# Attention scores by head on half the partitions, and value products of the first units in 32-column pieces, in an attention plus feed-forward kernel

## The chip, the cores and the metric

The kernel runs on one core of a Trainium2 chip. The metric is the device time of one execution in microseconds (us); the time before is the median of three runs. A profile is one execution taken by the hardware profiler. In it PE is TensorE (PEld its weight loads), DVE is VectorE, ACT is ScalarE, POOL is GpSimd and SP is SyncE, whose queue issues all the DMAs here.

## The reference

Chunked attention with a few memory keys, and behind it a two-layer feed-forward net on the result. Everything is float32.

```python
B, H, S, D = 4, 8, 768, 64            # batch, heads, sequence, head size; chunk 32, left 16, right 8, n_mem 8
for c in range(S // 32):              # a chunk of 32 queries sees 8 memory keys and up to 56 keys around it
    k_full = concat([mem_k, k[:, :, l_start:r_end]]);  v_full = concat([mem_v, v[:, :, l_start:r_end]])
    scores = (q_c @ k_full.T) / sqrt(D)
    a = exp(scores - max(scores));  a = a / (sum(a) + 1e-9)
    out[:, :, c_start:c_end] = a @ v_full
x = out.transpose(0, 2, 1, 3).reshape(3072, 512)
h = x @ w_in                          # 512 x 2048
g = maximum(h, 0) + alpha * minimum(h, 0)
return g @ w_out                      # 2048 x 512
```

## The kernel before

The 3072 tokens are cut into 8 blocks of 384 (`BT`). A block has 4 attention **units**, each a pair of heads, so there are 32 units; a unit's result is 128 rows of x (two heads of 64) by 384 tokens. The feed-forward net works through 16 pieces `f` of the hidden size for each block. For a piece, `up` (L581) makes h of 128 hidden rows by 384 tokens in 12 matmuls, since each operand is split into a high and a low part and three of the four products are added; ACT and DVE bend it (`sides`, `join`, `high`, `low`), and `down` (L613) adds 9 matmuls of 128 by 512 to the block's output in three PSUM banks. These split products run in fp32r; the products of attention are plain float32.

A unit's **scores** (`score_products`, L269) are 12 matmuls: 4 groups `g` of 32 output partitions times 3 slots `n`. A chunk has 32 queries, so a matmul writes 32 partitions. Its moving operand is 128 columns, 64 keys for each of two heads. The keys lie in `kbs`, which has a plane for each head with zeros on the other head's 64 partitions, so one matmul over 128 rows gives both heads. The zeros are written once by memsets (L189, L190), and the keys come in two DMAs of 64 partitions each (`load_k`, L235).

The **first 8 units** (blocks 0 and 1, `windows`, L407) run before the feed-forward net has anything to do and go another way than the 24 later ones. DVE takes the maximum (L417) and subtracts it (L421), ACT exponentiates, DVE sums (L429), inverts (L435) and scales the weights (L438), TensorE transposes them into the bank `t_ps` (L445), ACT copies them out (L450), and 24 matmuls of 64 output columns make the **values** (`values`, L460) in `a_ps`. `xh` and `xl` (L386, L390) are the two parts of x. A few matmuls on a constant tile (`stir`, L254) stand ahead of scores and transposes. In the later units the scores are exponentiated in six pieces on ACT (L299), GpSimd scales (L318), DVE transposes in 32 x 32 squares (L339), and 8 matmuls make the values (L353).

The 8 PSUM banks: two for h, three for the output of a block (`o0`, `o1`, `o2` in `ps_o`), two for scores (`s0`, `s1` in `ps_s`), one for values (`a`). The first units' scores all use `s0` and their transposes `s1`; later units alternate between the two. Blocks 0 and 1 share the weights as these arrive (`ORDER`, `NJOINT`): block 1's first 9 pieces accumulate in `s0`, `s1` and `a`.

The order of the work is not the order of the code. Each step is handed to a planner (`Plan`) with its engine, an assumed cost, what it reads and writes, and a due time; the planner walks a list schedule and writes each engine's instructions in that order. A change of a cost, a key or a due time so moves instructions everywhere. A later unit begins at the feed-forward step that `BEGIN` or `LATER` names; its weights are due `DUE_WEIGHTS` steps on, and its values stand `DUE_VALUES` steps on. Weights of the net arrive as bit patterns and are decoded by ACT and DVE (`decode_part`, L523 to L550) before they can be used. All DMAs stand in SP's queue in the planner's order.

Of the kernel before, what the change touches and what calls it, by code (L numbers as in the profile page):

```python
# [78 lines left out]
BEGIN = {2: (2, 4, 6, 8)}  # L79
# [5 lines left out]
DUE_WEIGHTS, DUE_VALUES = 2, 4  # L85
# [67 lines left out]
def body(ctx: ExitStack, tc: tile.TileContext, qvw, kw, vw, w_in, w_out, alpha, out):  # L153
# [23 lines left out]
    kbs = [const.tile([P, 2, NT, NKT], F32, name=f"kb{i}") for i in range(NKB)]  # L177
# [3 lines left out]
    spare = [wps[f, 0].tile([P, 2 * NT * NKT + BT], F32, name="early", tag="w") for f in (NF - 1, NF - 2)]  # L181
    kbs += [t[:, :2 * NT * NKT].rearrange("p (h t k) -> p h t k", h=2, t=NT) for t in spare]
    qs = [const.tile([P, BT], F32, name=f"q{i}") for i in range(2)] + [t[:, 2 * NT * NKT:] for t in spare]
# [42 lines left out]
    def load_unit(u):  # L226
        blk, pr = divmod(u, NPAIR)
        state[u] = {}
        i = sets(u)

        def load_q():
            nc.sync.dma_start(out=qs[i], in_=qvw[blk, pr, :, :BT])

        def load_k(h2):
            nc.sync.dma_start(out=kbs[i][h2 * D:(h2 + 1) * D, h2], in_=kw[blk, pr, h2 * D:(h2 + 1) * D])  # L235

        step(SP, 0.75, load_q, writes=[("q", i)], rest=due(u))
        for h2 in range(2):
            step(SP, 0.55, partial(load_k, h2), writes=[("k", i, h2)], rest=due(u))
# [16 lines left out]
    def score_products(u):  # L256
        blk, pr = divmod(u, NPAIR)
        st = state[u]
        k = u % 2 if u >= NWIN else 0
        s_ps = ps_s.tile([P, 512], F32, name="s_ps", tag=f"s{k}")  # L260
        if u < NWIN:
            stir(s_ps, STIR[0] if u == 0 else STIR[1])
        st["s"] = s_ps[:, :NJ * 2 * KW].rearrange("p (n h k) -> p n h k", n=NJ, h=2)
        st["sg"] = s_ps[:, :NJ * 2 * KW].rearrange("p (n k) -> p n k", k=KW)
        for n in range(NJ):
            for g in range(4):
                t, j = SLOT[(g, n)]
                c = t * NJ + j
                nc.tensor.matmul(  # L269
                    out=st["s"][g * CH:(g + 1) * CH, n],  # L270
                    lhsT=qs[sets(u)][:, c * CH:(c + 1) * CH],
                    rhs=kbs[sets(u)][:, :, t, STARTS[j]:STARTS[j] + KW],
                    start=True, stop=True,
                )
# [9 lines left out]
    def scores(u):  # L284
        st = state[u]

        def top():
            hide(u)
            st["mx"] = sm.tile([P, NJ * 2], F32, name="mx", tag=f"mx{u % 3}")
            nc.vector.tensor_reduce(out=st["mx"], in_=st["sg"], axis=AX.X, op=ALU.max)  # L290
# [4 lines left out]
        def exps(i):  # L295
            if i == 0:
                st["e"] = at.tile([P, NJ * 2, KW], F32, name="e", tag=f"e{u % 2}")
                st["den"] = sm.tile([P, NJ * 2, 1], F32, name="den", tag=f"den{u % 3}")
            nc.scalar.activation(out=st["e"][:, i], in_=st["sg"][:, i], func=AF.Exp, scale=SCALE,  # L299
                                 bias=st["mx"][:, i:i + 1], accum_out=st["den"][:, i])  # L300

        step(DVE, 0.66, top, writes=[("s", u % 2), ("mx", u % 3)], rest=due(u))
        step(DVE, 0.16, negate, writes=[("mx", u % 3)], rest=due(u))
        for i in range(NJ * 2):
            step(ACT, 0.54, partial(exps, i), reads=[("s", u % 2), ("mx", u % 3)],
# [54 lines left out]
    def attend(place, olds, news):  # L360
# [11 lines left out]
        for u in news:  # L372
            reads += [("q", sets(u)), ("k", sets(u), 0), ("k", sets(u), 1)]
            writes += [("s", u % 2)]
        step(PE, 0.85 * len(olds) + 0.82 * len(news) - (0.2 if olds and news else 0.0), products, reads=reads, writes=writes,
# [25 lines left out]
    def load_windows(u):  # L401
# [5 lines left out]
        step(SP, 1.4, load, writes=vw_keys(u), rest=due(u))  # L407

    def windows(u):

        st = state[u]
        sk, tk = ("s", 0), ("s", 1)

        def top():
            hide(u)
            st["mx"] = sm.tile([P, NJ * 2, 1], F32, name="mx", tag=f"mx{u % 3}")
# [376 lines left out]
```

## Time and profile before

| | |
|---|---|
| runs | 622.9, 627.49, 624.33 us; median 624.33 |
| the profiled execution | 626.75 us, of which the span from the first to the last instruction is 625.0 |
| busy | PE 613.4 us (98%), PEld 538.2, DVE 404.1, ACT 261.6, POOL 25.0 |
| chain that ended last | PE 96%, DVE 2%; o_ps L613 43%, h_ps L581 42%, s_ps L269 4.1%, a_ps L353 3.1%, a_ps L460 1.8% |
| scores, all 32 units | L269 MATMUL, 672 + 96 records, 24.6 + 3.9 us busy |
| values, first 8 units | L460 MATMUL, 192 + 192 records, 6.8 + 6.4 us busy |

A float32 matmul leaves two records in the trace, so 12 matmuls of scores are 24 records. Matmul records overlap, since they are pipelined: what a block of them costs is read from the start of its first record to the start of what follows. A `[x <- y]` behind a row is the idle time of that engine before it, and who ended it.

### The profile page before, as it was taken

The page shows a single profiled execution, that of the slowest core. Times are in us where ns is not written, and L with a number is a line of the kernel's source. Part 1 is how long each engine was busy: PE and PEld are TensorE (multiplying, and loading weights), DVE is VectorE, ACT ScalarE, POOL GpSimd, SP SyncE. Part 2 cuts the span into 40 slices and gives each one's busy share as a digit, 9 for nine tenths or more (in the row PEclk, how much of TensorE's full clock was granted, in tenths as well). Part 3 has the DMA queues.
Part 4 walks back from the last instruction along what each step waited for, and adds up shares of the span by engine and source line. Part 5 has one row for each costly group of instructions (what it writes and reads, how often), then busy time and mean ns, then how long its engine had stood idle before and what let it go on. Part 6 is the DMA issues. An engine that isn't in the chain of part 4 may idle for free.

```text
span 625.0 us, 10996 instructions
## 1 busy us (share of the span) xinstructions
PE 613.4 (98%) x4278; PEld 538.2 (86%) x4278; DVE 404.1 (65%) x984; ACT 261.6 (42%) x716; POOL 25.0 (4%) x37
## 2 busy tenths in 40 slices
PE   6999999999999999999999999999999999999997
PEld 3688999988888889988888988888998888988996
DVE  6788888976975676665566665567666556633332
ACT  2478989764423323433324323342334332231212
POOL 1001000001000000000000000000000000000000
PEclk9898999999999999999999999999999999999999
DMA  8999800022312100311111111130013100010001
GB/s 231 283 404 409 277 1 1 2 62 73 122 46 71 47 29 21 99 49 49 47 46 54 48 49 47 48 99 23 27 49 98 49 18 18 2 51 1 2 0 50
DMA packets 22596, 48.43 MB, mean 77 GB/s; under 512 B 3088, under 2 KB 7184, under 8 KB 22544
## 3 DMA queue, kind: packets, MB, share of 16 engines
q1 hardware_dynamic: 22544, 47.73, 23.7%
q8 instruction: 33, 0.54, 0.4%
q14 instruction: 19, 0.16, 0.1%
HBM read 41.43 MB, written 6.29 MB: 76 GB/s over the span
## 4 chain that ended last, share of the span: by engine, by line
PE 96%; DVE 2%; issue 0%; ACT 0%
PE o_ps L613 43%; PE h_ps L581 42%; PE s_ps L269 4%; PE a_ps L353 3%; PE a_ps L460 2%; PE s_ps L254 1%; DVE pt L339 1%; PE t_ps L445 0%; PE t_ps L254 0%; DVE a L539 0%; ACT w_t L531 0%; DVE up L595 0%; DVE w L550 0%; DVE mx L417 0%; DVE w_t L535 0%
## 5 line engine op out<-in xcount | busy, mean ns | idle before, releaser
L581 PE MATMUL h_ps<-xh,w 128*128 128x384 f32 x1024 | 262.6, 337 | 0.9 <-DVE w L550 0.9
L613 PE MATMUL o_ps<-w,gh 128*128 128x512 f32 x768 | 239.8, 394 | 0.0
L581 PEld LDWEIGHTS h_ps<-xh,w 128*128 128x128 f32 x1024 | 186.7, 189 | 4.7 <-DVE w L550 1.2
L581 PE MATMUL h_ps<-xl,w 128*128 128x384 f32 x512 | 174.0, 340 | 0.5 <-DVE xl L390 0.5
L613 PEld LDWEIGHTS o_ps<-w,gh 128*128 128x128 f32 x768 | 144.1, 188 | 27.8
L591 ACT ACTIVATE up<-h_ps 128x384 f32<-128x384 f32 x128 | 63.2, 493 | 222.0 <-PE h_ps L581 217.6
L613 PE MATMUL o_ps<-w,gl 128*128 128x512 f32 x384 | 151.7, 395 | 0.1
L595 DVE SCALAR_TENSOR_TENSOR up<-dn,nal,up 128x384 f32<-128x384 f32 x128 | 79.3, 620 | 107.0 <-ACT dn L591 106.3
L339 DVE STREAM_TRANSPOSE pt<-e 32x192 f32<-32x192 f32 (+1 forms) x336 | 99.5, 301 | 9.8 <-POOL e L318 5.3
L581 PEld LDWEIGHTS h_ps<-xl,w 128*128 128x128 f32 x512 | 96.6, 189 | 5.9 <-ACT xh L386 0.8
L613 PEld LDWEIGHTS o_ps<-w,gl 128*128 128x128 f32 x384 | 72.1, 188 | 15.9 <-issue 3.6
L605 DVE TENSOR_TENSOR gl<-up,gh 128x384 fp32r<-128x384 f32 x128 | 71.2, 557 | 3.9 <-ACT gh L601 0.3
L591 ACT ACTIVATE dn<-h_ps 128x384 f32<-128x384 f32 x128 | 62.4, 488 | 0.0
L299 ACT ACTIVATE e<-s_ps,mx 128x64 f32<-128x64 f32 x144 | 43.2, 319 | 36.3 <-DVE mx L293 35.4
L601 DVE CAST gh<-up 128x384 fp32r<-128x384 f32 x104 | 36.5, 352 | 22.7 <-PE o_ps L613 16.8
L386 ACT CAST xh<-a_ps 128x384 fp32r<-128x384 f32 x32 | 15.3, 479 | 58.1 <-PE a_ps L353 50.0
L318 POOL TENSOR_TENSOR e<-e,den 128x384 f32<-128x384 f32 x24 | 20.3, 847 | 462.5 <-DVE den L315 438.8
L299 ACT ACTIVATION_READ_ACCUMULATOR e<-s_ps,mx 128x1 f32 x144 | 30.4, 211 | 0.0
L312 DVE TENSOR_SCALAR den<-den 128x6 f32<-128x6 f32 x24 | 4.1, 169 | 32.1 <-ACT e L299 32.1
L269 PE MATMUL s_ps<-kb,q 128*32 128x128 f32 x672 | 24.6, 280 | 0.0
L353 PEld LDWEIGHTS a_ps<-pt,v_t 128*64 128x64 f32 x384 | 16.6, 136 | 8.7 <-issue 8.7
L269 PEld LDWEIGHTS s_ps<-kb,q 128*32 128x32 f32 x672 | 17.2, 111 | 5.5 <-issue 2.1
(59 smaller groups left out, 312.2 us busy)
## 6 DMA issues: line engine op xcount, KB each, us to landing
w_t<-w_in SPq DMA_DIRECT2D x16, 512.0 KB, 10.1
w_t<-w_out SPq DMA_DIRECT2D x16, 512.0 KB, 10.0
kb<-kw SPq DMA_DIRECT2D x56, 136.0 KB, 3.1
v_t<-qvw SPq DMA_DIRECT2D x24, 256.0 KB, 2.7
out<-o_t SPq DMA_DIRECT2D x24, 256.0 KB, 2.1
q<-qvw SPq DMA_DIRECT2D x28, 192.0 KB, 3.1
vw<-vw SPq DMA_DIRECT2D x4, 384.0 KB, 6.6
early<-vw SPq DMA_DIRECT2D x4, 384.0 KB, 6.6
```

The source lines that it names most:

```text
L269: nc.tensor.matmul(out=st["s"][g * CH:(g + 1) * CH, n], lhsT=qs[sets(u)][:, c * CH:(c + 1) * CH], rhs=kbs[sets(u)][:, :, t, STARTS[j]:STAR ...
L299: nc.scalar.activation(out=st["e"][:, i], in_=st["sg"][:, i], func=AF.Exp, scale=SCALE, bias=st["mx"][:, i:i + 1], accum_out=st["den"][:, i])
L318: nc.gpsimd.tensor_tensor(out=st["e"], in0=st["e"], in1=st["den"].broadcast_to([P, NJ * 2, KW]), op=ALU.mult)
L339: nc.vector.transpose(out=pts[u % NPT][quad * CH:(quad + 1) * CH, j, t0:t0 + n1 - n0].rearrange("p t h q -> p (t h) q"), in_=(st["e"], zer ...
L353: nc.tensor.matmul(out=st["a"][h2 * D:(h2 + 1) * D, t * TQ:(t + 1) * TQ], lhsT=st["v"][:, t, h2, :], rhs=pts[u % NPT][:, :, t, h2, :], sta ...
L386: nc.scalar.copy(out=st["xh"], in_=st["a"][:, :BT])
L581: nc.tensor.matmul(out=h["ps"][:, :BT], lhsT=ws[f, 0][:, wk, k * P:(k + 1) * P], rhs=xs[first + k][xk], start=(k == 0 and n == 0), stop=(k ...
L591: nc.scalar.activation(out=h[name], in_=h["ps"][:, :BT], func=AF.Relu, scale=sign)
L595: nc.vector.scalar_tensor_tensor(out=h["g"], in0=h["dn"], scalar=nal[:, f:f + 1], in1=h["up"], op0=ALU.mult, op1=ALU.add)
L601: copy(out=h["gh"], in_=h["g"])
L605: nc.vector.tensor_tensor(out=h["gl"], in0=h["g"], in1=h["gh"].bitcast(F32), op=ALU.subtract)
L613: nc.tensor.matmul(out=o_ps[tt], lhsT=h[gk][:, tt * P:(tt + 1) * P], rhs=ws[f, 1][:, wk], start=(f == first_f and i == 0), stop=(f == last ...
```

## The change

It has these parts. (1) Scores go by head: 24 matmuls of 64 columns instead of 12 of 128, each on the 64 partitions of its head, without zeros; the two heads write two different PSUM banks (a tile of `[P, 2, 512]`). (2) `kbs` loses its second plane and the memsets, and a unit's keys come in one DMA on 128 partitions. (3) The first units' scores alternate between two pairs of banks, `ps_s` and the first two banks of `ps_o`, and their transposes use the third bank of `ps_o`; so block 0's first `down` has to wait for the last of these. Later units have one pair of banks in place of two single ones. (4) The first units' value products write 32 output columns at a time, 48 matmuls instead of 24. (5) The first units' weights are scaled by GpSimd instead of DVE. (6) The planner's costs and due times change: block 2's units begin one step later, weights are due one step later.

```diff
-BEGIN = {2: (2, 4, 6, 8)}
+BEGIN = {2: (3, 5, 7, 9)}
...
-DUE_WEIGHTS, DUE_VALUES = 2, 4
+DUE_WEIGHTS, DUE_VALUES = 3, 4
...
-    kbs = [const.tile([P, 2, NT, NKT], F32, name=f"kb{i}") for i in range(NKB)]
+    kbs = [const.tile([P, NT, NKT], F32, name=f"kb{i}") for i in range(NKB)]
...
-    for i, kb in enumerate(kbs):
-        eng = nc.gpsimd if i % 2 else nc.vector
-        eng.memset(kb[0:D, 1], 0.0)
-        eng.memset(kb[D:P, 0], 0.0)
...
-        def load_k(h2):
-            nc.sync.dma_start(out=kbs[i][h2 * D:(h2 + 1) * D, h2], in_=kw[blk, pr, h2 * D:(h2 + 1) * D])
-
-        step(SP, 0.75, load_q, writes=[("q", i)], rest=due(u))
-        for h2 in range(2):
-            step(SP, 0.55, partial(load_k, h2), writes=[("k", i, h2)], rest=due(u))
+        def load_k():
+            nc.sync.dma_start(out=kbs[i], in_=kw[blk, pr])
+
+        step(SP, 0.65, load_q, writes=[("q", i)], rest=due(u))
+        step(SP, 0.81, load_k, writes=[("k", i)], rest=due(u))
...
-        k = u % 2 if u >= NWIN else 0
-        s_ps = ps_s.tile([P, 512], F32, name="s_ps", tag=f"s{k}")
+        pair = (ps_o if u < NWIN and u % 2 else ps_s).tile([P, 2, 512], F32, name="s_ps", tag="s")
...
-                nc.tensor.matmul(
-                    out=st["s"][g * CH:(g + 1) * CH, n],
-                    lhsT=qs[sets(u)][:, c * CH:(c + 1) * CH],
-                    rhs=kbs[sets(u)][:, :, t, STARTS[j]:STARTS[j] + KW],
-                    start=True, stop=True,
-                )
+                for h2 in range(2):
+                    rows = slice(h2 * D, (h2 + 1) * D)
+                    nc.tensor.matmul(
+                        out=st["s"][g * CH:(g + 1) * CH, n, h2],
+                        lhsT=qs[sets(u)][rows, c * CH:(c + 1) * CH],
+                        rhs=kbs[sets(u)][rows, t, STARTS[j]:STARTS[j] + KW],
+                        start=True, stop=True,
+                    )
...
-            nc.vector.tensor_tensor(out=st["e"], in0=st["e"], in1=st["den"].broadcast_to([P, NJ * 2, KW]),
+            nc.gpsimd.tensor_tensor(out=st["e"], in0=st["e"], in1=st["den"].broadcast_to([P, NJ * 2, KW]),
...
-            st["t"] = ps_s.tile([P, 512], F32, name="t_ps", tag="s1")
+            st["t"] = ps_o.tile([P, 512], F32, name="t_ps", tag="a")
...
-                    for h2 in range(2):
+                    for h2, i in ((0, 0), (1, 0), (0, 1), (1, 1)):
                         rows = slice(h2 * D, (h2 + 1) * D)
                         nc.tensor.matmul(
-                            out=st["a"][rows, c * CH:(c + 1) * CH],
-                            lhsT=vws[u % NSET][rows, c, :],
+                            out=st["a"][h2 * D + i * CH:h2 * D + (i + 1) * CH, c * CH:(c + 1) * CH],
+                            lhsT=vws[u % NSET][rows, c, i * CH:(i + 1) * CH],
                             rhs=st["et"][rows, n, g * CH:(g + 1) * CH],
```

The planner's costs that change with it: a unit's scores 1.26 to 1.08 (first units) and 0.82 to 0.67 (later), values of the first units 1.55 to 0.95, scaling from DVE 0.55 to POOL 0.86, and the loads.

Place one, TensorE among the first units: the scores and values around the first transposes. Before:

```order
L254 MATMUL s_ps<-busy 128x512
L269 MATMUL s_ps<-early 32x128 x12
L460 MATMUL a_ps<-et,vw_162 64x32 x24
L254 LDWEIGHTS busy
L254 MATMUL t_ps<-busy 128x512
L445 MATMUL t_ps<-eye,e 128x128 x3
```

The same place in the changed kernel, where the fifth unit's scores stand ahead of the second unit's values:

```order
L249 MATMUL s_ps<-busy 128x512
L264 MATMUL s_ps<-kb_154,q_159 32x64 x24
L455 MATMUL a_ps<-et,vw_162 32x32 x48
L249 LDWEIGHTS busy
L249 MATMUL s_ps<-busy 128x512
```

Both blocks have twice the matmuls at half the size, and scores of the next units have moved ahead of transposes by about one unit.

Place two, DVE among the first units, from one unit's sum to the next unit's. Before, the scaling (L438) stands in DVE's row:

```order
L432 TENSOR_SCALAR den<-den 128x6
L280 MEMSET s_ps 32x2x16
L417 TENSOR_REDUCE mx<-s_ps 128x6
L435 RECIPROCAL den<-den 128x6
L421 TENSOR_TENSOR e<-s_ps,mx 128x384
L438 TENSOR_TENSOR e<-e,den 128x384
L429 TENSOR_REDUCE den<-e 128x6
```

Of the change, a little later, where the decoding of the net's first weights (L530, L534) stands between the units' steps:

```order
L427 TENSOR_SCALAR den<-den 128x6
L530 TENSOR_SCALAR w_t<-w_t 128x512
L430 RECIPROCAL den<-den 128x6
L534 SCALAR_TENSOR_TENSOR a<-a,w_t 128x512
L416 TENSOR_TENSOR e<-s_ps,mx 128x384
```

And GpSimd's whole row in the changed kernel from its first work on:

```order
L187 MEMSET eye 128x128
L188 ISA
L188 AFFINE_SELECT eye<-eye 128x128
L433 TENSOR_TENSOR e<-e,den 128x384 x8
L479 MEMSET e_1111 128x384
L482 MEMSET pt_1113 128x768
```

The eight scalings left DVE; behind a reciprocal, where GpSimd now starts, DVE goes on with whatever is next, here a decode step with two operands in SBUF. GpSimd's memsets of the later units' buffers stand behind the eight scalings.

Place three, TensorE at block 0's first `down`, with the numbers of the tiles (`o_ps_1033` is the pair of banks, `o_ps_1034` the third one, `t_ps_1015` and `a_ps_1051` belong to the last of the first units):

```order
L440 MATMUL t_ps_1015<-eye_156,e_844 128x128 x3
L609 MATMUL o_ps_1033<-w_941,gl_1023 128x512
L609 MATMUL o_ps_1033<-w_941,gh_1012 128x512 x2
...
L609 MATMUL o_ps_1034<-w_941,gl_1023 128x512
L609 MATMUL o_ps_1034<-w_941,gh_1012 128x512 x2
L455 MATMUL a_ps_1051<-et_1028,early_163 32x32 x48
```

Before, at the same place:

```order
L445 MATMUL t_ps_759<-eye_156,e_683 128x128 x3
L581 MATMUL h_ps_639<-xl_768,w_505 128x384
L581 MATMUL h_ps_639<-xh_764,w_505 128x384 x2
L613 MATMUL o_ps_780<-w_752,gl_770 128x512
L613 MATMUL o_ps_780<-w_752,gh_755 128x512 x2
L613 MATMUL o_ps_781<-w_752,gl_770 128x512
```

The first `down` stands behind the last transpose in both kernels; one quarter of an `up` has moved from ahead of it to behind the last values.

More of the change, by code (lines that the diff above doesn't have):

```diff
@@ L298, in exps @@
                 st["den"] = sm.tile([P, NJ * 2, 1], F32, name="den", tag=f"den{u % 3}")
-            nc.scalar.activation(out=st["e"][:, i], in_=st["sg"][:, i], func=AF.Exp, scale=SCALE,
-                                 bias=st["mx"][:, i:i + 1], accum_out=st["den"][:, i])
-        step(DVE, 0.66, top, writes=[("s", u % 2), ("mx", u % 3)], rest=due(u))
+            nc.scalar.activation(out=st["e"][:, i], in_=st["s"][:, i // 2, i % 2], func=AF.Exp, scale=SCALE,
+                                 bias=st["mx"][:, i // 2, i % 2:i % 2 + 1], accum_out=st["den"][:, i])
+        step(DVE, 0.66, top, writes=["s", ("mx", u % 3)], rest=due(u))
         step(DVE, 0.16, negate, writes=[("mx", u % 3)], rest=due(u))
         for i in range(NJ * 2):
-            step(ACT, 0.54, partial(exps, i), reads=[("s", u % 2), ("mx", u % 3)],
+            step(ACT, 0.54, partial(exps, i), reads=["s", ("mx", u % 3)],
                  writes=[("e", u % 2, i), ("den", u % 3, i)] if i else e_keys(u) + den_keys(u), rest=due(u))
@@ L372, in attend @@
         for u in news:
-            reads += [("q", sets(u)), ("k", sets(u), 0), ("k", sets(u), 1)]
-            writes += [("s", u % 2)]
-        step(PE, 0.85 * len(olds) + 0.82 * len(news) - (0.2 if olds and news else 0.0), products, reads=reads, writes=writes,
+            reads += [("q", sets(u)), ("k", sets(u))]
+            writes.append("s")
+        step(PE, 0.85 * len(olds) + 0.67 * len(news) - (0.2 if olds and news else 0.0), products, reads=reads, writes=writes,
              rest=rest(place))
@@ L465, in values @@
                         )
-        step(PE, 1.26, partial(score_products, u), reads=[("q", sets(u)), ("k", sets(u), 0), ("k", sets(u), 1)],
+        step(PE, 1.08, partial(score_products, u), reads=[("q", sets(u)), ("k", sets(u))],
              writes=[sk], rest=due(u))
@@ L474, in windows @@
         step(DVE, 0.19, inverse, writes=den_keys(u))
-        step(DVE, 0.55, scale, reads=den_keys(u), writes=e_keys(u))
+        step(POOL, 0.86, scale, reads=den_keys(u), writes=e_keys(u))
         step(PE, 0.68, turn, reads=e_keys(u) + ["eye"], writes=[tk], rest=due(u, 1))
         step(ACT, 0.48, keep, reads=[tk], writes=["e2"])
-        step(PE, 1.55, values, reads=["e2"] + vw_keys(u), writes=["a"], rest=due(u, 1))
+        step(PE, 0.95, values, reads=["e2"] + vw_keys(u), writes=["a"], rest=due(u, 1))
         split(u)
@@ L500, in load @@
             nc.sync.dma_start(out=raw[k][:, j].rearrange("p m b -> p (m b)"), in_=srcs[i][f])
-        after = {NF - 1: [("q", 2), ("k", 2, 0), ("k", 2, 1)], NF - 2: [("q", 3), ("k", 3, 0), ("k", 3, 1)],
+        after = {NF - 1: [("q", 2), ("k", 2)], NF - 2: [("q", 3), ("k", 3)],
                  NF - 3: [("vw", 2), ("vw", 3)]}.get(f, [])
         for i in range(2):
-            step(SP, 1.9, partial(load, i), writes=[("r", f, i)] + after, rest=rest(place_of(f)))
+            step(SP, 1.31, partial(load, i), writes=[("r", f, i)] + after, rest=rest(place_of(f)))
     def place_of(f):
@@ L608, in down @@
             if f == first_f:
-                banks = [(ps_o, f"o{i}") for i in range(NTT)] if not joint else [(ps_s, "s0"), (ps_s, "s1"), (ps_a, "a")]
-                o_ps.extend(pool.tile([P, DM], F32, name="o_ps", tag=tag) for pool, tag in banks)
+                pair = (ps_s if joint else ps_o).tile([P, 2, DM], F32, name="o_ps", tag="s")
+                last = (ps_a if joint else ps_o).tile([P, DM], F32, name="o_ps", tag="a")
+                o_ps.extend([pair[:, 0], pair[:, 1], last])
             for tt in range(NTT):
@@ L649, in keep @@
         for tt in range(NTT):
-            step(ACT, 0.58, partial(copy, tt), reads=[(("s", 0), ("s", 1), "a")[tt]],
+            step(ACT, 0.58, partial(copy, tt), reads=[("s", "s", "a")[tt]],
                  writes=[("tmp", tt)], rest=rest(PLACE[1, NJOINT - 1] + 1))
@@ L669, in store @@
             place = PLACE[blk, NF - 1] + 1
-            step(DVE if blk == 1 else ACT, 0.68 if blk == 1 else 0.59, partial(copy, tt, t, o), reads=["o"],
+            step(DVE if blk == 1 else ACT, 0.68 if blk == 1 else 0.59, partial(copy, tt, t, o), reads=["os", "oa"],
                  writes=[("tmp", t)], rest=rest(place))
```

29 lines of the change are left out of this document (14 added, 15 removed).

## The prediction

> **What bounds the kernel now.** I read the page first, then what TensorE waited for, then the stretches of the span.
>
> ```profile
> span 625.0 us, 10996 instructions
> PE 613.4 (98%) x4278; PEld 538.2 (86%) x4278; DVE 404.1 (65%) x984; ACT 261.6 (42%) x716; POOL 25.0 (4%) x37
> PE   6999999999999999999999999999999999999997
> PEclk9898999999999999999999999999999999999999
> PE 96%; DVE 2%; issue 0%; ACT 0%
> ```
>
> TensorE is busy from end to end, and the chain that ended last is 96% TensorE; the only slices with less than 9 tenths of clock are the second and the fourth, which is the time of the first units. Where does it stand still?
>
> ```profile
> engine line waited for: us in total, times, longest us
> PE s_ps L254 <- DVE e L421: 2.9, 2, 1.4
> ...
> PE a_ps L460 <- issue: 1.2, 1, 1.2
> PE h_ps L581 <- DVE w L550: 0.9, 1, 0.9
> ```
>
> The last of these ends the matter:
>
> ```profile
> 48.68 1.22 DVE L550 TENSOR_TENSOR w<-a,w 128x1024 fp32r<-128x1024 f32 x1
> 49.96 0.62 PE L581 MATMUL h_ps<-xh,w 128*128 128x384 f32 x2 [0.94 <-DVE w L550]
> ```
>
> At 49.96 us TensorE waits for VectorE to finish decoding the third pair of weights, and after that it never waits again. So the kernel has two parts. **Behind 50 us** the end is simply TensorE's work laid end to end: every microsecond taken from it comes off the time. **Ahead of 50 us** the question is when that third pair is ready and the work before it done, and there several engines are tight:
>
> ```profile
> core 0: us, PE busy (x) PEld busy (x) DVE busy (x) ACT busy (x) POOL busy (x), PEclk, DMA share, GB/s
> 25.00:30.00 5.00, 4.04 (x51) 2.80 (x55) 3.05 (x6) 2.33 (x5) 0.00 (x0) 0.66 1.05 260
> 45.00:50.00 5.00, 4.07 (x60) 3.11 (x58) 5.00 (x8) 4.52 (x8) 1.22 (x3) 1.00 1.03 407
> sum 45.00, PE 38.61 PEld 29.81 DVE 35.09 ACT 23.82 POOL 1.22; mean PE 4.29 PEld 3.31 DVE 3.90 ACT 2.65 POOL 0.14
> ```
>
> The sum is over nine stretches from 5 to 50 us: TensorE 38.6, VectorE 35.1 of 45, and the DMA engines full (the share in each row is about 1).
>
> **The later units' scores (24 units, behind 50 us).** One unit, and inside it the first records:
>
> ```profile
> 127.01 0.86 PE L269 MATMUL s_ps<-kb,q 128*32 128x128 f32 x24
> 127.81 0.50 PE L613 MATMUL o_ps<-w,gl 128*128 128x512 f32 x1
> 127.00:127.04 0.04, 0.03 (x4) 1.00 0.00 0
> 127.04:127.14 0.10, 0.10 (x4) 1.00 0.00 0
> 127.14:127.17 0.03, 0.03 (x8) 1.00 0.00 0
> ```
>
> A block costs 127.81 - 127.01 = 0.80 us. The number behind x counts the records in flight, so it shows the starts: four within 0.04 us, none for 0.1 us, four more by 127.17. Four records on four different groups of output partitions run beside each other, and such a group holds TensorE some 0.11 us. Six groups make 0.66, and 0.14 is left for getting in and out.
>
> The change makes 48 records of 64 columns. If both heads run beside each other as the four groups of partitions do, there are again six groups, of eight records and half the columns: 6 x 0.055 + 0.14 = 0.47 us, **0.33 less**. At the other end the heads take turns and a group gets no shorter than the shortest in this trace, the 0.06 us of the first units' values (their row follows): 12 x 0.06 + 0.14 = 0.86, **0.06 more**. I take 0.25 less, nearer the row of the scores, which shows concurrency across tiles of the array, and short of the best because eight starts in 0.055 us would be as dense as the four in 0.04. 24 x 0.25 = **6.0 us**; the ends are -1.4 and +7.9.
>
> **The first units' values and scores on TensorE.**
>
> ```profile
> 13.60 1.59 PE L460 MATMUL a_ps<-et,vw 64*64 64x32 f32 x48 [0.57 <-ACT et L450]
> 15.12 0.39 PE L254 MATMUL t_ps<-busy 128*128 128x512 bf16 x1
> 13.59:13.61 0.02, 0.01 (x2) 1.00 1.69 461
> 13.61:13.67 0.06, 0.06 (x2) 1.00 1.15 329
> 13.67:13.69 0.02, 0.02 (x4) 1.00 1.03 307
> ```
>
> Values cost 15.12 - 13.60 = 1.52 us: 24 pairs, one of each head, a pair each 0.06 us. With 32 output columns there are 96 records. If four of them run together in half a pair's time, 24 x 0.03 + 0.1 = 0.82, 0.70 less; if still only two do, 48 x 0.03 + 0.1 = 1.54, nothing. I take 0.55 less, since pairs of both heads already overlap in this row. With the scores, TensorE is relieved of 8 x (0.25 + 0.55) = 6.4 us ahead of 50 us.
>
> [...] The values write both heads' row halves into one bank, before and after, while the scores get two banks. [...]
>
> **VectorE and GpSimd ahead of 50 us.**
>
> ```profile
> L438 DVE TENSOR_TENSOR e<-e,den 128x384 f32<-128x384 f32 x8 | 4.4, 550 | 0.0
> 139.67 0.62 DVE L595 SCALAR_TENSOR_TENSOR up<-dn,nal,up 128x384 f32<-128x384 f32 x1
> 141.67 0.83 POOL L318 TENSOR_TENSOR e<-e,den 128x384 f32<-128x384 f32 x1 [6.38 <-DVE den L315]
> 141.76 1.16 DVE L595 SCALAR_TENSOR_TENSOR up<-dn,nal,up 128x384 f32<-128x384 f32 x1 [0.23 <-ACT dn L591]
> ```
>
> VectorE loses eight scalings, 4.4 us. GpSimd takes 0.83 for one, so a unit's own chain is 0.28 longer, which the neighbouring unit's steps cover. And it costs something: the same operation of VectorE on two SBUF operands takes 0.62 alone and 1.16 beside GpSimd's scaling. In the changed order three of the eight scalings start just ahead of a decode step of that kind (L534), so 3 x 0.54 = 1.6 comes back and VectorE is relieved of 2.8 us; at worst all eight, 4.3, and nothing is left. GpSimd's later memsets now stand behind eight scalings, but they wait for the last values anyway. In SP's queue the keys now stand ahead of the queries, and the first weights of the net ahead of the fifth unit's loads: at most one load of 0.5 MB more ahead of a unit, 1.9 us at the 280 GB/s of the rows below, and at most that much less ahead of the decoding; both lie within the ends of the next number.
>
> TensorE's 6.4 and VectorE's 2.8 are the two relieved limits of the same stretch, and either can be last. I take **4.5 us** for the point at 49.96, the middle. The ends are -1.3 (two more stalls, below) and 8.4 (data, below).
>
> **What costs nothing, and its cover.** The key planes' memsets (four on VectorE, four on GpSimd) lie beside the eight stirring matmuls, which fill TensorE to 1.46 + 3.60 = 5.06 us (the first row below); without that cover the first scores would still wait for their loads. The one pair of score banks makes a unit wait for the exponentials of the one before, and later value products wait for the squares turned under a later due time:
>
> ```profile
> 1.46 3.60 PE s_ps L254 x8
> 58.39 4.12 PE o_ps L613 x18
> L450 ACT COPY et<-t_ps 128x384 f32<-128x384 f32 x8 | 4.0, 497 | 2.5 <-PE t_ps L445 2.5
> 216.86 0.33 ACT L299 ACTIVATE e<-s_ps,mx 128x64 f32<-128x64 f32 x1
> 221.82 3.16 DVE L339 STREAM_TRANSPOSE pt<-e 32x192 f32<-32x192 f32 x11
> 230.81 0.88 PE L353 MATMUL a_ps<-pt,v_t 128*64 128x96 f32 x16
> 231.63 0.32 PE L269 MATMUL s_ps<-kb,q 128*32 128x128 f32 x4
> ```
>
> The last exponential of a unit ends at 217.2 and the next scores start at 231.63: 14 us of room. The last square ends at 225.0, 5.8 us ahead of the values. Only block 2's units stand closer, and they begin a step later. If the room went, up's and down's matmuls queued behind the attention step would wait too, and each microsecond would count 24 times. The first `down` now waits for the last transposes to be copied; but in both orders it stands behind them, and six matmuls into the pair of banks, at 4.12 / 18 = 0.23 us each, cover the copy of 0.5.
>
> **Sum.** 6.0 + 4.5 = 10.5 us. The profiled execution took 626.75 (span 625.0 and 1.75 around it), 2.4 above the median of 624.33. So it would be 616.3, and 613.8 by the median: I forecast **614**.
>
> **The rivals.**
>
> *Data come sooner: 610.* The loads ahead of 32 us against those behind it:
>
> ```profile
> DMA packets 3411, 7.57 MB, mean 280 GB/s; under 512 B 473, under 2 KB 1244, under 8 KB 3409
> DMA packets 3290, 11.36 MB, mean 406 GB/s; under 512 B 493, under 2 KB 493, under 8 KB 3285
> kb<-kw SPq DMA_DIRECT2D x56, 136.0 KB, 3.1
> ```
>
> With the engines full in both (5 to 32 us, and 32 to 60), the first moves 280 GB/s and the second 406. Only the first is full of the keys' half loads, on 64 partitions each. If they are the brake, 7.57 MB take 18.6 us instead of 27, and the data of the first units no longer hold anything back: the front moves by 8.4, to 624.33 - 6.0 - 8.4 = 610. Against it: smaller packets are slower too, and there are as many of them after. [...]
>
> *The heads take turns: 622.* The change then does not do what it says. Scores cost 0.06 more, 24 times 1.4 us, and the front moves by some 3.5: 624.33 + 1.4 - 3.5. For it: two heads share the same output partitions, which no record of before does. Against it: the values' pairs.
>
> *The front eats its gain: 620.* TensorE's instructions grow, and the row of 1.2 us "issue" among its waits is one stall in which none came; the clock of 0.66 in the stretch after it means 3.4 of 5 us at half speed, some 1.7 us lost. Two more of these cost 5.8, 1.3 more than the 4.5 gained: 624.33 - 6.0 + 1.3.
>
> *Slower: 642.* A group might be held by its weight load and not by its columns:
>
> ```profile
> L269 PEld LDWEIGHTS s_ps<-kb,q 128*32 128x32 f32 x672 | 17.2, 111 | 5.5 <-issue 2.1 <-DVE warm L195 0.9
> ```
>
> The load takes 0.111, as long as a group. Then 64 columns cost what 128 did, and if the heads also take turns a block is 12 x 0.11 + 0.14 = 1.46, 0.66 more: 24 x 0.66 = 15.8, with some 2 in front, 642. It decides from 0.07 us per group, where 24 x 0.19 eats the front's gain, and is slower by over 1% from 0.09. Against it: the values' 64-column loads follow each other in 0.06.
>
> **How the numbers follow.** Forecast 0.50 (610 to 618), data sooner 0.17, turns 0.15, front eaten 0.13, slower 0.05. A measurement here tells about 1%, 6.2 us, from no change: faster means below 618.1. That is nearly all of the first two and a part of the fourth, 0.66; slower 0.05; the rest, 0.29, is within 1%. The range runs from 607, where the data come sooner and the scores reach their best end halfway, to 622, which takes in the turns and the eaten front; what is left out is the slower rival and the tails.
>
> **What would show it.** A block of later scores from 0.80 to 0.55 us, starts in groups of eight; 0.86 speaks for turns, 1.4 for the weight load. Values of the first units from 1.52 to about 1.0. TensorE's last wait for VectorE's L545 at 45.5 instead of 49.96; nearer 42 speaks for the data, with more than 350 GB/s ahead of 32 us. Decode steps of 1.1 us and more beside GpSimd. I would be wrong if TensorE waited anywhere behind 60 us, or if half-speed stretches took the place of its work in front.

## The result, and the profile after

The changed kernel takes **633.56 us** (four runs, 631.34 to 633.67) against 623.66 for the kernel before on the same chip: 1.0138 of it, with an interval of 1.009 to 1.0186, so slower by 1.4%. I had forecast 614, faster. The profiled execution took 633.67 us with a span of 631.9, 6.9 more than the span before. (One kernel below, with the later units' scores alone, took 635 to 640 us in eight of its twelve runs; its comparison leaves those out, and no trace explains them.)

The page after, with TensorE's busy time, the slices, the granted clock, the instruction packets and the chain that ended last:

```profile
span 631.9 us, 13240 instructions
PE 610.7 (97%) x5423; PEld 537.8 (85%) x5430; DVE 399.1 (63%) x972; ACT 260.7 (41%) x716; POOL 32.1 (5%) x41
PE   6687999999999999999999999999999999999997
PEclk9587999999999999999999999999999999999999
q8 instruction: 42, 0.69, 0.5%
PE 95%; issue 2%; DMA 1%; SPq 1%; DVE 1%; ACT 0%; ACTq 0%; DVEq 0%
```

Behind the fourth slice TensorE is full at full clock, as before. The loss is in slices one to four, the time of the first units. What TensorE waited for, in us, times, longest:

```profile
PE a_ps L455 <- issue: 6.4, 3, 3.8
PE s_ps L264 <- issue: 4.5, 5, 2.6
PE s_ps L249 <- DVE warm L191: 1.5, 1, 1.5
PE a_ps L455 <- ACT et L445: 1.2, 2, 0.6
```

"issue" was 1.5 us before and is 10.9 now: TensorE stood in the middle of a block of matmuls, waiting for nothing that the profile names. The same waits in the timeline, where such a row is the rest of a block behind its stall:

```profile
13.44 0.93 PE L455 MATMUL a_ps<-et,vw 64*32 64x32 f32 x85 [1.01 <-issue]
...
19.47 0.46 PE L264 MATMUL s_ps<-kb,q 64*32 64x64 f32 x12 [2.58 <-issue]
...
23.43 0.68 PE L264 MATMUL s_ps<-kb,q 64*32 64x64 f32 x31 [0.81 <-issue]
...
42.76 0.76 PE L455 MATMUL a_ps<-et,vw 64*32 64x32 f32 x40 [1.62 <-issue]
57.46 0.33 PE L455 MATMUL a_ps<-et,early 64*32 64x32 f32 x6 [3.78 <-issue]
```

The last one holds up the end of the front: 90 of 96 records of a block had run, the other 6 came 3.8 us later. The two stretches of the front, before:

```profile
5.00:32.00 27.00, 22.07 (x442) 16.23 (x442) 19.45 (x53) 8.93 (x19) 0.00 (x0) 0.94 1.03 280
32.00:60.00 28.00, 26.54 (x268) 22.91 (x268) 22.92 (x45) 23.58 (x38) 1.78 (x3) 0.94 1.03 406
```

and after (span, then busy time and records of PE, PEld, DVE, ACT and POOL, then clock, DMA share, GB/s):

```profile
5.00:32.00 27.00, 18.16 (x667) 12.58 (x653) 15.26 (x42) 7.83 (x16) 4.46 (x5) 0.68 0.81 296
32.00:60.00 28.00, 21.41 (x588) 17.40 (x577) 18.71 (x38) 17.97 (x29) 4.79 (x6) 0.80 0.98 373
```

TensorE's matmul records have risen from 710 to 1255, its busy time has fallen by 9 us, and the granted clock is 0.68 and 0.80 instead of 0.94. The trace's records of the clock hold only full and half speed, so a clock of 0.68 over 27 us is 17 us at half speed; by these records it is 30.7 us in all, 6.8 before.

The blocks that the change was to shorten did become shorter. Values of a first unit without a stall, and later scores:

```profile
31.80 1.02 PE L455 MATMUL a_ps<-et,early 64*32 64x32 f32 x96
32.75 0.44 PE L576 MATMUL h_ps<-xl,w 128*128 128x384 f32 x1
...
313.28 0.72 PE L264 MATMUL s_ps<-kb,q 64*32 64x64 f32 x48
313.93 0.50 PE L609 MATMUL o_ps<-w,gl 128*128 128x512 f32 x1
```

Values take 0.95 us instead of 1.52, scores 0.65 instead of 0.80 (over all 24 later blocks 0.655 instead of 0.798, so 24 x 0.14 = 3.4 us). The front's loss can be read from the net's own matmuls, which are the same 2688 in both kernels: the 100th starts at 62.9 us before and at 71.9 after, the last at 621.0 and 627.2. So the front lost 9.1 us, and 2.8 of them came back in the later units; the 0.6 up to the span's 6.9 lie behind the last matmul. Of the 9.1 the waits are 8.6 (all of TensorE's waits add up to 16.4, before to 7.8). On the other side stand the values' eight times 0.57, 4.6, and the first units' scores, eight times 0.14, 1.1. What remains, some 6.2, I put down to the half speed; no run measures it by itself.

**What the stalls have in common.** Instructions are themselves fetched, as packets of the queue `q8 instruction`: 33 with 0.54 MB before (in its page), 42 with 0.69 MB after, 16 KB each. The records of PE and PEld grew by 2297, so if the nine more packets are TensorE's, a packet is 2297 / 9 = 255 of them. I counted how many records of TensorE stand ahead of the end of each stall of 0.36 us and more inside a block (not at its start), ahead of 64 us:

```
before                      691
changed                     440  693  946        1962  2472
values in 64 columns             693
scaling on VectorE               693  946  1200  1962  2472
before, values in 32        437  690  943  1449  1703  1957
weights held back           440  693  946  1202  1962
before, dense dummies       439  693  947
```

(The rows below the second are kernels of the experiments.) All stand on one grid, 437 to 440 and then multiples of 253 to 256, whatever instruction is there. The other kernels below that stall keep to it within a few records (1201 and 1455; 697 and 949; 697; 443 and 697). And each such stall ends behind the packet of that number: in the changed kernel the one at 440 behind the first packet, those at 693 and 946 behind the second and third, at 1962 the seventh, at 2472 the ninth. These five packets start at 11.0, 17.1, 21.0, 40.4 and 55.0 us, and each stall ends 2.4 to 2.5 us later; in all kernels it is 2.3 to 2.8. TensorE stops where a packet ends, because the next one is late. Between the first and the last stall of the changed kernel lie eight packets and 44 us. The packets that start beside full DMA engines, behind 33 us (a share of 0.96 to 1.04 from 35 to 60 us), stand 5.6 to 7.8 us apart, although each is under way for only 1.0 to 1.1 us; those from 21 to 29 us, where the data pause, 3.7 to 3.9. That pause, in five of these microseconds:

```profile
25.00:30.00 5.00, 4.02 (x128) 2.81 (x135) 3.35 (x8) 2.92 (x7) 0.00 (x0) 0.50 0.26 66
```

### The profile page after: what moved, and what is told of

It is laid out like the page before. It is cut to its first block, busy times and chain, and to the rows that moved or that the text cites. A ratio compares the mean times of both kernels' runs of the same rounds, so it can differ in the third digit from the quotient of the medians.

```text
span 631.9 us, 13240 instructions
## 1 busy us (share of the span) xinstructions
PE 610.7 (97%) x5423; PEld 537.8 (85%) x5430; DVE 399.1 (63%) x972; ACT 260.7 (41%) x716; POOL 32.1 (5%) x41
## 4 chain that ended last, share of the span: by engine, by line
PE 95%; issue 2%; DMA 1%; SPq 1%; DVE 1%; ACT 0%; ACTq 0%; DVEq 0%
PE h_ps L576 44%; PE o_ps L609 43%; PE s_ps L264 3%; PE a_ps L348 3%; PE a_ps L455 1%; DMA early<-qvw 1%; PE t_ps L440 1%; PE t_ps L249 0%; SPq L231 0%; PE s_ps L249 0%; SPq L228 0%; DVE e L416 0%; ACT et L445 0%; ACT o_t L656 0%; DVE w L545 0%
## 5 line engine op out<-in xcount | busy, mean ns | idle before, releaser
L334 DVE STREAM_TRANSPOSE pt<-e 32x192 f32<-32x192 f32 (+1 forms) x336 | 101.1, 302 | 19.7 <-POOL e L313 14.2
L609 PEld LDWEIGHTS o_ps<-w,gl 128*128 128x128 f32 x384 | 72.1, 188 | 13.7
L313 POOL TENSOR_TENSOR e<-e,den 128x384 f32<-128x384 f32 x24 | 22.1, 922 | 460.4 <-DVE den L310 460.4
L381 ACT CAST xh<-a_ps 128x384 fp32r<-128x384 f32 x32 | 15.3, 478 | 28.8 <-PE a_ps L455 14.6
L264 PE MATMUL s_ps<-kb,q 64*32 64x64 f32 x1344 | 21.4, 229 | 4.8 <-issue 4.1
L264 PEld LDWEIGHTS s_ps<-kb,q 64*32 64x32 f32 x1344 | 16.3, 109 | 10.4 <-issue 6.6
L385 DVE TENSOR_TENSOR xl<-a_ps,xh 128x384 fp32r<-128x384 f32 x32 | 17.7, 552 | 8.5 <-ACT xh L381 8.4
L317 ACT COPY e<-e 128x192 f32<-128x192 f32 x24 | 8.5, 353 | 34.4 <-POOL e L313 34.3
```

The costliest lines, as they stand in the source:

```text
L264: nc.tensor.matmul(out=st["s"][g * CH:(g + 1) * CH, n, h2], lhsT=qs[sets(u)][rows, c * CH:(c + 1) * CH], rhs=kbs[sets(u)][rows, t, STARTS[ ...
L313: nc.gpsimd.tensor_tensor(out=st["e"], in0=st["e"], in1=st["den"].broadcast_to([P, NJ * 2, KW]), op=ALU.mult)
L334: nc.vector.transpose(out=pts[u % NPT][quad * CH:(quad + 1) * CH, j, t0:t0 + n1 - n0].rearrange("p t h q -> p (t h) q"), in_=(st["e"], zer ...
L385: nc.vector.tensor_tensor(out=xl, in0=st["a"][:, :BT], in1=st["xh"].bitcast(F32), op=ALU.subtract)
L609: nc.tensor.matmul(out=o_ps[tt], lhsT=h[gk][:, tt * P:(tt + 1) * P], rhs=ws[f, 1][:, wk], start=(f == first_f and i == 0), stop=(f == last ...
```

## The experiments

Theory A is that: packets arrive too slowly for the first units' denser stream. B puts the gaps down to GpSimd's scaling, C to the faster data loads.

### Values back in 24 matmuls

```diff
-                    for h2, i in ((0, 0), (1, 0), (0, 1), (1, 1)):
-                            out=st["a"][h2 * D + i * CH:h2 * D + (i + 1) * CH, c * CH:(c + 1) * CH],
+                    for h2 in range(2):
+                            out=st["a"][rows, c * CH:(c + 1) * CH],
```

> The changed kernel with one part undone: the first units' values in 24 matmuls of 64 output columns again, not 48 of 32; 768 fewer instructions on TensorE ahead of 60 us. Theory A (TensorE's instructions come in packets of 256, and the denser stream of the first units uses them up faster than they arrive): of the stalls named 'issue' (9.8 us inside blocks in the changed kernel) those inside the values go, 6.4 us (1.01, 1.62, 3.78), while each unit's values cost 0.57 us more; half-speed time falls from 30.7 us to 10 to 20; 624 to 628. Theory B (GpSimd's longer scaling opens the gaps): nothing that matters changes, 632 to 637. Theory C (the data loads, now at 400 GB/s, crowd the instruction packets out, however many there are): the stalls stay in number and length and move into other blocks, 630 to 636.

Measured: 623.03, 0.9951 of before (0.9923 to 0.9979). TensorE's waits:

```profile
PE a_ps L455 <- issue: 2.2, 1, 2.2
PE s_ps L264 <- DMA early<-qvw: 1.8, 3, 1.3
```

One stall of the five is left, and half speed is down to 10.2 us. This one part of the change cost 1.9% of the time, though each of its blocks is 0.57 us shorter. That is A, a little under its range; B is out, and so is C in the form that the number of instructions does not matter. That the stalls inside the values would be the ones to go did not come true: the one that stayed, at record 693, is now inside the values, and those at 440, 946, 1962 and 2472 are gone.

### Scaling back on VectorE

```diff
-            nc.gpsimd.tensor_tensor(out=st["e"], in0=st["e"], in1=st["den"].broadcast_to(...), op=ALU.mult)
+            nc.vector.tensor_tensor(out=st["e"], in0=st["e"], in1=st["den"].broadcast_to(...), op=ALU.mult)
```

> The changed kernel with one part undone: the first units' weights are scaled by VectorE again. TensorE's instructions and the loads stay. Theory A (instruction packets): the stalls by 'issue' stay at 8 to 11 us, 631 to 636. Theory B (GpSimd's longer scaling opens the gaps): the stalls or the half-speed time fall by half or more, 623 to 628. Theory C (data loads crowd the packets out): as A, 631 to 636.

Measured: 635.74, 1.0161 (1.0125 to 1.0198); stalls by "issue" of 13.6 us in the blocks, more than any theory had. B is refuted. Whether GpSimd's scaling is worth the 2 us between this and the changed kernel the intervals do not tell.

### The kernel before with 32-column values alone

The first diff the other way round, in the kernel before.

> The kernel before with one part of the change alone: the first units' values in 48 matmuls of 32 output columns. 768 more instructions ahead of 60 us, loads as before (about 280 GB/s ahead of 32 us, full speed behind). Theory A (instruction packets): 2 to 4 us of new stalls by 'issue', those behind 32 us above all, a half-speed stretch or two more, 626 to 630. Theory B (GpSimd's scaling): no stalls; the values' 0.57 us per unit show in part, 620 to 623. Theory C (data loads at 400 GB/s in the first 20 us): no new stalls ahead of 32 us, 621 to 625.

Measured: 632.84, 1.0121 (1.0096 to 1.0145), more than any theory had. The first three of its stalls, in the values:

```profile
18.35 1.31 PE L460 MATMUL a_ps<-et,vw 64*32 64x32 f32 x91 [2.42 <-issue]
...
24.76 1.06 PE L460 MATMUL a_ps<-et,early 64*32 64x32 f32 x90 [1.90 <-issue]
...
31.44 0.96 PE L460 MATMUL a_ps<-et,early 64*32 64x32 f32 x89 [2.09 <-issue]
```

They come at 288 to 307 GB/s too, beside half loads that keep the engines' share at 0.86 to 1.05 (15 to 35 us). So C in the form "400 GB/s crowds them out" falls: the stalls are there at the lower rate, with the engines about as full. From the first of its stalls (18.35) to the last (56.42) lie six packets, 6.3 us each.

### The same instructions beside idle DMA engines

```diff
-            step(SP, 1.31, partial(load, i), writes=[("r", f, i)] + after, rest=...)
+            step(SP, 1.31, partial(load, i), reads=["hold"] if f >= 3 else [], writes=[("r", f, i)] + after, rest=...)
...
+        nc.scalar.copy(out=raw[k].bitcast(F32)[:, 0, 0:1, 0], in_=state[u]["et"][:, 0, 0:1])   # u = 7, k = (3, 0)
```

> The changed kernel, but the loads of the net's fourth pair of weights and all later ones wait until the transposed scores of the last first unit are copied (about 50 us); so the DMA engines are idle from about 38 us to there, and the same instructions of TensorE run beside no load. Theory A, if the packets come late only because they stand behind data in the DMA engines, and theory C: the stalls at 41 us (1.62) and 53.7 us (3.78, or its half if loads are back by then) go, and with them a half-speed stretch; 625 to 630. Theory A, if the instructions alone outrun the fetch: the stalls stay, 632 to 636. Theory B: the stalls stay, 632 to 636. By any of them the fourth pair, which lands at about 58 us, may come too late for the net; then VectorE's decoding shows among TensorE's waits behind 60 us, with up to 5 us.

Measured: 625.95, 0.9999 of before (0.9974 to 1.0023) where the changed kernel has 1.0138, so 1.4%, some 8.7 us, won by loading later. DMA traffic from 38 to 58 us, of the changed kernel:

```profile
q1 hardware_dynamic: 2217, 8.10, 101.6%
q8 instruction: 3, 0.05, 1.0%
```

and of this one (packets, MB, share of the engines):

```profile
q1 hardware_dynamic: 1342, 3.49, 47.8%
q8 instruction: 4, 0.07, 1.6%
```

The packets now start at 40.1, 43.8, 47.6 and 51.5 us, 3.7 to 3.9 apart instead of 5.6 to 7.8. The stall at record 1962, at 42 us just after the traffic ends, is still 1.14 us; that at 2472, 3.78 us long, is gone, and so are both half-speed stretches behind 40 us. The stalls ahead of 40 us, beside loads as before, are still there and even longer (3.37 us at record 693), so "issue" still adds up to 8.6 us:

```profile
PE s_ps L265 <- issue: 6.3, 4, 3.4
PE a_ps L456 <- issue: 2.3, 3, 1.1
```

By names and shapes TensorE's matmuls stand in the same order in both traces up to 61.6 us, behind the last of the first units; only there has the planner moved a `down`. So the same instructions ran without the stall at 2472. This shows the cause as A has it with the second half of C: packets come late beside data. That they wait behind the data in the DMA engines is the likely reading; the trace does not tell when a packet was asked for.

### Only instructions added: spread, and dense

Spread, behind each pair of value matmuls of the kernel before:

```diff
+                        for _ in range(2):
+                            nc.tensor.matmul(out=st["a"][rows, BT:BT + 1], lhsT=busy[rows, :D], rhs=busy[rows, :1], ...)
```

> The kernel before with nothing but instructions added: behind each of the first units' value products (64 output columns, as before) stand two matmuls of one column on a constant tile, into a column that nobody reads; 96 more instructions a unit, as many as the 32-column pieces add, 768 in all. Theory A (TensorE's instructions come in packets of 256, too slowly beside full DMA engines): stalls by 'issue' of 8 to 13 us ahead of 60 us and more half-speed time, 630 to 640, as in the kernel before with the 32-column values (632.8). Rival: it was the 32-column form itself (its tiles, its banks) that stalled; then the added instructions cost their issue alone, 0.8 us a unit at most and in part hidden, 624 to 630, without stalls by 'issue' beyond the 1.5 of before.

Measured: 635.64, 1.0172 (1.0135 to 1.0209), but with 1.9 us of stalls by "issue" (at records 1201 and 1455): the expected time for another reason. The dummies did not run beside the values, so that a block took 3.96 us at half speed (15.02 to 18.98) and a unit 7.4 us, as long as a packet takes to come. The time went into 20.5 us at half speed and into the blocks:

```profile
15.00:20.00 5.00, 4.98 (x100) 4.73 (x101) 2.36 (x7) 1.00 (x2) 0.00 (x0) 0.50 1.04 296
20.00:25.00 5.00, 5.00 (x91) 3.70 (x90) 1.91 (x5) 1.00 (x2) 0.00 (x0) 0.50 1.03 296
```

TensorE is busy throughout, at a clock of 0.50. The half-speed stretch begins at 9.9 us, though, ahead of the first dummy at 15.3, so this run does not show what set it off. So I asked again with dummies that issue back to back, on four tiles of the array, behind the block:

```diff
+            for m in range(48):
+                rows, cols = ...                      # four tiles in turn
+                nc.tensor.matmul(out=st["a"][cols, BT + m:BT + m + 1], lhsT=busy[rows, :CH], rhs=busy[rows, :1], ...)
```

> The kernel before with instructions added, now dense: behind each first unit's 24 value matmuls stand 48 of one column on a constant tile, spread over four tiles of the array so that they issue back to back (96 more instructions a unit, some 0.8 us); the values themselves are untouched. Theory A (packets too slow for the stream): stalls by 'issue' of 5 to 12 us, at the dummies or behind them, 632 to 640. Rival, after the run with spread dummies (which stalled only 1.9 us in all): the number of instructions does not matter, only the 32-column values stall; then 0.8 us a unit at most, 6.4 in all and part of it hidden, 625 to 631, with stalls by 'issue' below 2.5.

Measured: 636.35, 1.0191 (1.0139 to 1.0243), with these stalls:

```profile
19.95 1.47 PE L460 MATMUL a_ps<-et,vw 64*64 64x32 f32 x43 [0.36 <-issue]
25.88 1.47 PE L460 MATMUL a_ps<-et,early 64*64 64x32 f32 x42 [1.81 <-issue]
32.35 2.45 PE L460 MATMUL a_ps<-et,early 64*64 64x32 f32 x41 [2.36 <-issue]
```

4.5 us, a little under my range but well over the rival's 2.5, and 13.7 us at half speed, of which 6.8 lie ahead of the first dummies (16.9 us). A block of dummies itself holds TensorE for 0.43 us, 3.4 in all, so not all of the 10 us more are stalls. One of the four executions took 642.82 us at a granted clock of 1.0: the loss does not need half speed. The stalls stand inside the untouched 64-column values, at records 439, 693 and 947. The form of the matmuls is not what stalls; the count is.

### Keys in half loads, and weights paced

In the kernel with 64-column values, the keys in two loads again, and in another run the weights behind a wait at 15 us (made as the hold above, for all loads but the first):

```diff
-            nc.sync.dma_start(out=kbs[i], in_=kw[blk, pr])
+            for h2 in range(2):
+                nc.sync.dma_start(out=kbs[i][h2 * D:(h2 + 1) * D], in_=kw[blk, pr, h2 * D:(h2 + 1) * D])
```

> The changed kernel with the values in 64-column pieces and with a unit's keys in two loads of 64 partitions each, as before; all else, the order on TensorE too, stays. If the half loads were the brake of the first 30 us: the rate ahead of 20 us falls from 400 to about 290 GB/s, the first units wait for their data (2 to 5 us more of waits named DMA), 624 to 629. If they were not: the rate stays near 400 and the time at 623. If data that come more slowly leave room for the instruction packets: the stall by 'issue' of 2.15 us shrinks, and the time stays at 621 to 624 in spite of the slower data.

Measured: 626.11, 1.0007 (0.9982 to 1.0032) where whole loads gave 0.9951. From 10 to 15 us, whole, then half:

```profile
10.00:15.00 5.00, 3.59 (x105) 3.06 (x106) 3.33 (x8) 2.04 (x4) 1.66 (x2) 1.00 1.03 400
```

```profile
10.00:15.00 5.00, 2.63 (x102) 1.67 (x102) 2.84 (x10) 0.84 (x2) 1.66 (x2) 1.00 0.99 289
```

The engines are full both times, at 400 and 289 GB/s, so the half loads were the brake of the first 20 us. TensorE's waits for DMA rose from 2.2 to 4.4 us. But sooner data are worth only 0.56%, 3.5 us. The stall at the second packet shrank from 2.15 to 0.76 us, and one of 1.48 came at the third, so slower data did not make the packets come in time.

> The changed kernel with the values in 64-column pieces (623.0 us, with one stall by 'issue' of 2.15 at 17.4 us and half speed from 19 to 26 us), and the loads of the net's weights behind the first half pair wait until the second unit's transposed scores are copied (about 15 us), so that less data stands in the DMA engines between 12 and 17 us. Theory A with C (packets are late because they stand behind data): the second packet comes sooner than at 17.2, the stall shrinks below 1 us, the half-speed stretch goes or moves, 617 to 622. If instructions alone set the packets' times: the stall stays, 622 to 626. The last first units' data come some 4 us later in either case, which may cost up to 2 us.

Measured: 623.81, 0.9967 (0.994 to 0.9994); the stall stays at 2.0 us. The hold moved too little: the engines still carried 400 and 406 GB/s from 10 to 20 us. It tells nothing between the two theories.

### More stirring

```diff
-STIR = (8, 2, 1)
+STIR = (8, 4, 3)
```

> The changed kernel with the values in 64-column pieces (623.0; one stall of 2.15 us, half speed for 10.2 us behind it), with two more stirring matmuls ahead of each first unit's scores and of each transpose: 16 x 2 x 0.23 = 7.4 us more of work on TensorE, which fits where it waits. If the half-speed stretch comes from too little work in the windows before it and can be kept off by more: half-speed time from 10.2 to 3.4 or less, 3.4 us won and up to 7.4 us of work added: 620 to 626. If the stall alone makes it (TensorE has no instructions to run): the 10.2 stay or move, and the added work shows, 626 to 631.

Measured: 625.73, 0.9988 (0.9971 to 1.0006). The page's clock is full throughout:

```profile
PEclk9999999999999999999999999999999999999999
```

Half speed went from 10.2 us to nothing, the stalls stayed (1.9), and the time rose by 0.4%. Here the half-speed time was bought off with work on TensorE, at about its price. Stalls of the same kind stand without it, so half speed is not their cause; whether a stall sets off each half-speed stretch stays open.

### The later scores alone, and the front as before

The kernel before with scores by head in the 24 later units only; both banks became one buffer in this edit:

```diff
+    spair = ps_s.tile([P, 2, 512], F32, name="s_ps", tag="s")
...
+        if u >= NWIN:                                  # 24 matmuls by head, as in the change, rhs=kbs[...][rows, h2, ...]
...
+        s_ps = spair[:, 0]                             # first units' scores; their transposes use spair[:, 1]
```

> The kernel before with one part of the change alone: the 24 later units' scores go by head into two banks (with the later due times that belong to it); the first units, their loads, their scaling and the keys with zero planes stay. A block of later scores takes 0.65 instead of 0.80 us, 24 x 0.15 = 3.6 us. Theory A (instruction packets, front only): the front stays as before, so 3.6 less than before, 619 to 622. Rival: the denser stream stalls the later units too, or the one pair of banks and the later due times cost what they gain; then 623 to 627, and TensorE waits behind 60 us.

Measured: 0.9998 (0.9966 to 1.003). TensorE waits for nothing behind 62 us, but in front the first units' values now wait for the copy of the transposes:

```profile
PE a_ps L474 <- ACT et L464: 4.0, 5, 1.4
```

before it was 0.6, and the 3.4 more are about what the later units gain. That is a fault of this edit.

> The kernel with the later scores by head alone, once more, with a look at one execution: of its twelve runs four took 624.1 to 625.7 and eight 635.0 to 640.0, while its front has the instructions of before. Theory A: in the long ones an early wait makes TensorE miss an instruction packet, so that stalls by 'issue' or half-speed stretches ahead of 60 us hold the 10 us; the later units are alike in both. Rival: the long ones lose it behind 60 us, in the later units, whose scores are the only thing changed. If this execution is one of the short ones, nothing is learnt.

This execution took 623.05, so nothing is learnt: why most of the earlier ones took 10 us more stays open, as no trace shows one. The cleaner form is the changed kernel with the first units' instructions of before:

```diff
+        if u < NWIN:                                   # 12 matmuls of 128 columns on keys with zero planes, in one bank
...
+            for h2 in range(2):
+                nc.sync.dma_start(out=kbs[i][h2 * D:(h2 + 1) * D, h2], in_=kw[blk, pr, h2 * D:(h2 + 1) * D])
```

with the 64-column values.

> The changed kernel with the whole instruction stream of the first units as before: their scores in 12 matmuls of 128 columns on keys with zero planes (two loads of 64 partitions, memsets), their values in 24 of 64 columns. What stays of the change: later scores by head, alternating pairs of banks, scaling by GpSimd, due times. Theory A (instruction packets; the form of the matmuls does not matter): no stall by 'issue' over 1.5 us in all, at most two half-speed stretches of 3.4 us, and the later units' 3.6 us show in full: 617 to 622. Rival (the new banks, GpSimd's scaling or the due times have a price of their own): 623 to 628, with new waits for other engines.

Measured: **622.18, 0.9937** (0.991 to 0.9964), the lowest of all, though its interval overlaps that of the changed kernel with 64-column values. Its waits hold no "issue" at all:

```profile
PE s_ps L269 <- DMA early<-qvw: 3.8, 2, 2.1
PE s_ps L254 <- DVE busy L176: 1.5, 1, 1.5
PE s_ps L269 <- DMA q<-qvw: 0.7, 1, 0.7
PE a_ps L473 <- ACT et L463: 0.6, 1, 0.6
```

0.63% is 3.9 us, about the 3.4 of the later units. (By the traces the later units gain 2.9 and the front 2.5, but the execution of before that was traced is one with a stall of 1.2 us, 2.4 above the median.) The banks, GpSimd's scaling and the due times carry no price that shows. What is left in front is mostly the half loads' slower data: 4.5 of the 6.5 us of waits.

## Why the prediction was wrong

The step that failed is the term of 4.5 us for the front. I took it as the middle between the work that TensorE (6.4) and VectorE (2.8) would be rid of, as if TensorE's instructions were always there when their turn comes. Measured, the front lost 9.1 us, because they were not. I had this only as the rival "the front eats its gain", with 0.13 and 620, priced as "two more" stalls of the one kind in the profile. Its mechanism was the right one; its size was 9.4 us more of stalls and 23.9 us more at half speed (up to 12 us lost, counted as the rival counts it), not 5.8 us together. The information was there: the one "issue" of 1.2 us in the profile before ends at record 691, at a packet's end, and the change adds nine packets to 33. I asked what a block of matmuls costs, never how fast its instructions can arrive. And by taking the stall as one row to be doubled, I left the slower side to a mechanism (weight loads) whose price did not come.

- *Later scores*: mis-sized. 0.14 us a unit and not 0.25, so 3.4 by the blocks and 2.8 by the net's matmuls for a forecast of 6.0, within the ends. The heads do run beside each other: the first 32 records start 6 to 10 ns apart, but for one gap of 33. Behind a pause of 85 ns the last 15 start every 13 ns on average, in many places every 16 to 17, which my groups of eight did not have in them. What sets that pace is not shown. Neither turns (0.86) nor the weight load (1.46) came.
- *Values*: right, 0.95 for a forecast of about 1.0. The two row tiles (the two heads' halves of the array's rows) write different partitions of one bank, and of the block at 31.80 us 16 records had started within 0.15 us, where of the block at 13.60 us before 8 had within 0.22. But the relief of TensorE that I counted from it was bought with instructions, and these were the scarce thing.
- *The front's gain of 4.5*: wrong in sign, 9.1 lost. VectorE's last wait ended at 39.4 us, ahead of the 45.5 that I had named, but the values stalled to 57.5 behind it.
- *GpSimd's collisions*: smaller than assumed. One decode step of 128x512 at L534 took 1.20 us beside a scaling, where I had three; in return three of the eight scalings took 0.95 to 1.27 us instead of 0.83.
- *Data come sooner*: right as a mechanism, worth 3.5 us and not 8.4. The sign I had named, more than 350 GB/s ahead of 32 us, came only ahead of 20 us (353 to 406); from 20 to 30 the loads pause, and 5 to 32 us has 296. With the keys in whole loads the engines moved 400 GB/s from 10 to 15 us and in half loads 289, at a share of 1.03 and 0.99; why the half loads are the slower ones no run shows.
- *Cover*: held. TensorE does not wait once behind 62 us, so one pair of banks and the later due times cost nothing there.

## What to carry to other kernels

Count instructions as well as work: here TensorE had a packet of about 255 records every 5.6 to 7.8 us beside full DMA engines, and the step that took a block of values from 1.52 to 0.95 us by doubling its instructions cost 1.9% of the time, since the stretch held more packets than came in time. An "issue" wait in the middle of a block was the sign; count the records ahead of it, and if such waits lie a packet apart, take instructions out or move data loads away. Ask which part of a change earns: scores by head paid in the later units, where TensorE does not wait once behind 62 us, and cost in front.

## What the runs showed of the hardware

- Instruction packets started 5.6 to 7.8 us apart beside full DMA engines (changed kernel, behind 33 us), and 3.7 to 3.9 us apart beside quiet ones (changed kernel from 21 to 29 us, and the one with loads held back from 40 to 52), while the changed kernel's from 11 to 61 us were under way for only 0.9 to 1.3 us each.
- A stall on the grid of about 254 records ended 2.3 to 2.8 us behind the start of a packet, in all eleven traces that have such stalls.
- Small matmuls on different tiles of the array (a block of later scores at 313.28 us, changed kernel) started 6 to 10 ns apart for 32 records (one gap of 33), then, behind a pause of 85 ns, one every 13 ns on average.
- Half-speed stretches lasted multiples of 3.41 us (3.41, 6.83, 10.24, 17.07 and 20.48 in these runs). What sets a stretch off is not settled here: with spread dummies the clock stayed at 0.50 from 15 to 25 us while TensorE was busy for 9.98 of the 10 us.
